# Weights in fp32 over SyncE's queue with casts on chip, in place of casting transfers from GpSimd, in a fused linear-attention and feed-forward kernel

## The chip, the cores and the metric

One Trainium2 chip, one of its cores. The metric is the device time of one execution in microseconds; a kernel's time is the median of its runs. TensorE (PE in the profile) multiplies matrices into PSUM; VectorE (DVE), ScalarE (ACT) and GpSimd (POOL) work on tiles of 128 partitions; SyncE (SP) computes nothing and issues transfers. Each of these engines takes its instructions strictly in the order in which they stand in the program: one that waits holds up all behind it. SyncE's transfers run over the queue that the page calls q1 hardware_dynamic, GpSimd's over q0 software_dynamic; both use the same 16 DMA engines. Only the transfers from GpSimd's queue change the type of the data in this kernel.

## What is computed

Gated linear attention (called GLA here) over a sequence, and a feed-forward layer on its output:

```python
# q, k, v, alpha: (4, 8, 768, 48) fp32
for t in range(S):
    state = alpha[:, :, t, :, None] * state + einsum('bhd,bhe->bhde', k[:, :, t], v[:, :, t])
    y[:, :, t] = einsum('bhd,bhde->bhe', q[:, :, t], state)
x = y.transpose(0, 2, 1, 3).reshape(3072, 384)
h = x @ w_in                 # w_in (384, 2048) fp32
r = maximum(h, 0)
out = (r * r) @ w_out        # w_out (2048, 384) fp32; out (3072, 384) fp32
```

The products are made in bf16 with sums in fp32, so both weights have to lie in SBUF as bf16: `w_in_b` (128 x 3 x 2048) and `w_out_b` (128 x 16 x 384). In HBM each is 3.15 MB of fp32.

## The kernel before, in words

The 3,072 rows are cut into 24 chunks of 128 rows, six to a sequence. For each chunk four fp32 loads of 192 KB (alpha, q, k, v: tiles `at`, `qt`, `kt`, `vt`, function `add_load`, line L290) go over SyncE's queue; each of the four tiles has six buffers, so the load of chunk s waits until chunk s - 6 has been used.

A chunk's GLA (`add_chunk`) is a chain over four engines. ScalarE takes Ln of alpha (L312); TensorE sums it over the rows (p0, `bank<-L_s,utri_b`); ScalarE makes A, its inverse and the end-of-chunk factors (L331 to L341); VectorE multiplies q and k with them (L350, L353); TensorE transposes (L220) and VectorE copies the result out (`qkT`, L307); TensorE makes the scores (`sc`), VectorE masks them (`sm`, L391, two a chunk); TensorE adds the chunk's share to the state (`st`), VectorE decays it (L411), ScalarE copies it to bf16 (`sb`, L416); TensorE makes the output (`bank<-vb,sm` and `bank<-sb,qkT`), ScalarE copies it (`xn`, L305), TensorE transposes it, and VectorE puts it into `xT_big` (L307). GpSimd casts v (`vb`, L317).

The feed-forward layer goes over groups of chunks, of 4, 1, 1, 2, 2, ... chunks. For a group and each of the 16 slices f of the hidden dimension, TensorE makes the first product from `w_in_b` (three matmuls; `add_moe1`), ScalarE the relu `r` (L490, eight buffers), VectorE the square `gT` (L497). The second product (`add_moe2`) takes `gT` and `w_out_b`, 16 matmuls for each chunk, in four quarters of four f; ScalarE or VectorE copies the result out (L527, L525) and SyncE stores it (L532). The first group starts its first four slices with three of its four chunks and adds the fourth chunk afterwards, and takes the first three quarters of the second product for all its four chunks before any last quarter. All matmuls go through one helper, L217.

The order of the instructions on each engine is written by a planner (`Plan`) when the kernel is built: every operation has an estimated duration, dependencies and a priority, and the planner puts them in the order of their planned starts. Some operations may go to the cheapest of several engines. Transfers have a planned queue of their own, `DMA`, which is served strictly in the order of adding. Changed durations thus change the order on every engine. Ahead of the first feed-forward work, gaps in TensorE's plan are filled with dummy matmuls (`bank<-warm`).

The weights come in nine pieces, `W_CUT`: w_in in slices of 2, 2, 4, 4, 4 of the 16 f, w_out in four slices of 4. Each is a transfer from GpSimd (L254, L256) that reads fp32 and writes bf16 into its place. Two kinds of holds keep the two queues apart: `hold_w` is a one-column copy on GpSimd that waits for a chunk load (q of chunk 3, later alpha of chunk 4) and so delays the weight transfers behind it, and `hold_x` is a one-column copy on GpSimd, from the first w_out piece into the alpha tile of chunk 4 (L275), for which SyncE's load of chunk 4 has to wait. The written order of loads and pieces is

```python
DMA_ORDER = [0, 1, 2, 3, "i", "i", "i", "i", "i", "o", "o", "o", 4, "o", 5]
LOAD_ORDER = {2: [(2, "at"), (2, "qt"), (2, "kt")], 3: [(3, "at"), (3, "qt"), (3, "kt"), (2, "vt"), (3, "vt")]}
HOLD_W = {3: "qt", 4: "at"}
HOLD_X = {4: ("o", 0)}
```

Of the kernel before, what the change touches and what calls it, by code (L numbers as in the profile page):

```python
# [8 lines left out]
FP32 = mybir.dt.float32  # L9
# [130 lines left out]
def kernel(  # L140
# [10 lines left out]
    nc = tc.nc  # L151
    B, H, S, D = q.shape
    HD = H * D
    P = 128
# [3 lines left out]
    d_model, d_ff = moe_w_in.shape  # L158
    n_tok = out.shape[0]
    KT = d_model // P  # L160
# [5 lines left out]
    w_in_r = moe_w_in.rearrange("(j p) f -> p j f", p=P)  # L166
    w_out_r = moe_w_out.rearrange("(j p) n -> p j n", p=P)
    out_r = out.rearrange("(tt p) n -> tt p n", p=P)

    consts = ctx.enter_context(tc.tile_pool(name="consts", bufs=1))  # L170
    big = ctx.enter_context(tc.tile_pool(name="big", bufs=1))
    LB = 6
    loads = ctx.enter_context(tc.tile_pool(name="loads", bufs=LB))
    work = ctx.enter_context(tc.tile_pool(name="work", bufs=4))
    rpool = ctx.enter_context(tc.tile_pool(name="rpool", bufs=8))
    opool = ctx.enter_context(tc.tile_pool(name="opool", bufs=6))

    ps_sc = ctx.enter_context(tc.tile_pool(name="ps_sc", bufs=1, space=PSUM))
    ps_st = ctx.enter_context(tc.tile_pool(name="ps_st", bufs=1, space=PSUM))
# [11 lines left out]
        out=utri_f, in_=utri_f, compare_op=ALU.is_ge, fill=0.0,  # L191
# [7 lines left out]
    w_in_b = consts.tile([P, KT, d_ff], BF16)  # L199
    w_out_b = consts.tile([P, FT, d_model], BF16)  # L200
# [12 lines left out]
    def pin(ins):  # L213
        tc.keep_in_program_order(ins)
# [18 lines left out]
        return banks[i].tile(shape, dt, name=f"bank{i}")  # L233
    X_SLACK = 0.2
    LD = 0.93
    WLD = 2.05
    SQ_PRIO = 0.0

    def add(eng, dur, emit, *deps, **kw):
        return plan.add(Op(eng, dur, emit, deps, **kw))  # L240

    w_ready = {"i": [], "o": []}
    W_CUT = {"i": [0, 2, 4, 8, 12, 16], "o": [0, 4, 8, 12, 16]}
    W_ISSUE = 0.78
    hold = consts.tile([P, 1], FP32)

    def load_w(which):
        j = len(w_ready[which])
        lo, hi = W_CUT[which][j:j + 2]

        def e_issue():
            if which == "i":
                sl = slice(lo * P, hi * P)
                pin(nc.gpsimd.dma_start(out=w_in_b[:, :, sl], in_=w_in_r[:, :, sl]))  # L254
            else:
                pin(nc.gpsimd.dma_start(out=w_out_b[:, lo:hi, :], in_=w_out_r[:, lo:hi, :]))  # L256
        issue = add("POOL", W_ISSUE, e_issue, w_gate[0], prio=-3.0, lat=0.4)
        w_ready[which].append(add("DMA", WLD * (hi - lo) / 4, lambda: None, issue, lat=2.2))

    def w_dep(which, f):  # L260
        return w_ready[which][[hi > f for hi in W_CUT[which][1:]].index(True)]

    w_gate = []

    def hold_w(d, nm):
        def e_hold():
            pin(nc.gpsimd.tensor_copy(hold, d[nm][:, 0, 0:1]))
        w_gate[:] = [add("POOL", 0.3, e_hold, d["ld_" + nm], prio=-6.0)]

    def hold_x(d, which, f):  # L270
        src = w_in_b[:, 0, f * P:f * P + 1] if which == "i" else w_out_b[:, f, 0:1]

        def e_hold():
            d["at"] = loads.tile([P, H, D], FP32, name="at")
            pin(nc.gpsimd.tensor_copy(d["at"][:, 0, 0:1], src))  # L275
        d["go"] = add("POOL", 0.3, e_hold, w_dep(which, f), prio=-6.0)

    C = [dict() for _ in range(NT)]
    state = {}
# [3 lines left out]
    def add_load(s, nm):  # L283
        d = C[s]
        b, c = divmod(s, NCH)

        def ld():
            if nm not in d:
                d[nm] = loads.tile([P, H, D], FP32, name=nm)
            pin(nc.sync.dma_start(out=d[nm], in_=SRC[nm][b, c]))  # L290
        prev = C[s - LB]["use_" + nm] if s >= LB else None
        d["ld_" + nm] = add("DMA", LD, ld, prev, d.get("go") if nm == "at" else None, lat=2.0 if s < 4 else 2.4, at=0.6)

    def add_chunk(s):
        d = C[s]
# [239 lines left out]

    DMA_ORDER = [0, 1, 2, 3, "i", "i", "i", "i", "i", "o", "o", "o", 4, "o", 5]
    LOAD_ORDER = {2: [(2, "at"), (2, "qt"), (2, "kt")], 3: [(3, "at"), (3, "qt"), (3, "kt"), (2, "vt"), (3, "vt")]}
    HOLD_W = {3: "qt", 4: "at"}
    HOLD_X = {4: ("o", 0)}
    for d in DMA_ORDER + [s for s in range(NT) if s not in DMA_ORDER]:  # L540
        if d in ("i", "o"):
            load_w(d)
        else:
            if d in HOLD_X:
                hold_x(C[d], *HOLD_X[d])
            for s, nm in LOAD_ORDER.get(d, [(d, nm) for nm, _ in srcs]):
                add_load(s, nm)
            if d == 3:
                add_chunk(2)
            if d != 2:  # L550
                add_chunk(d)
            if d in HOLD_W:
                hold_w(C[d], HOLD_W[d])
    b1 = b2 = None
    SPLIT_F = 4
    FIRST_PARTS = [[0, 1, 2], [3]]
# [38 lines left out]
    for op in plan.order:  # L595
        if op.eng == "PE":
# [3 lines left out]
            if pe_end is not None and DUMMY:  # L600
                n = max(0, int((op.start - pe_end - 0.2) / 0.11))
# [34 lines left out]
```

## Time and profile before

| | |
|---|---|
| runs | 195.91, 196.31, 198.04 us; median 196.31 |
| span of the profiled execution | 195.5 us, first to last instruction; the runs lie 0.4 to 2.5 us above it |
| TensorE busy | 183.6 us, 94% |
| VectorE, ScalarE busy | 133.8 us, 68%; 131.2 us, 67% |
| GpSimd busy | 24.9 us, 13% |
| q1 (SyncE) | 23.60 MB, its packets 55.7% of the 16 engines' span |
| q0 (GpSimd) | 3.15 MB as written (bf16), 11.5% |
| HBM read | 25.17 MB |
| DMA share by fortieths of the span | `6999999999989999989999968531101011011122`: nearly full until about 125 us, then low |

The page has no separate time for the profiled execution besides its span, so a sum is made on the span and set beside the runs. Busy time is the union of an engine's instructions; the share of the span is an average over stages that are limited by different things, so the prediction reads stretches of time as well as totals. A row of a timeline gives start, length, engine, line, operation, tiles written and read, shapes, and in brackets the idle time ahead of it with what ended it. A row of the chain gives start, length and what the time was spent on. A row of a stretch gives its bounds and length, each engine's busy time with its number of instructions (PE, PEld, DVE, ACT, POOL), the granted clock, the share of the DMA engines and the rate in GB/s.

### The profile page before, as it was taken

Reading aid. Unit: us, or ns where it says so; the run is one execution under the profiler, and the core shown is the slowest. Engines: PE = TensorE matmul, PEld = TensorE weight load, DVE = VectorE, ACT = ScalarE, POOL = GpSimd, SP = SyncE. Lnnn points to the kernel's source line nnn. Section 1 sums busy time; section 2 is a strip of 40 time slices with the busy share of each in tenths; the row PEclk is TensorE's granted clock in tenths of the full one; section 3 lists DMA queues with packets and bytes.
Section 4 is the critical chain, followed back from the end, with each engine's and each line's share of the span. In section 5 each row is a group of like instructions: output and inputs, shape, how many; then the busy total and the mean of one; then the engine's idle time right before and its main releaser. Section 6 shows DMA issues by size and latency. Waiting matters only on the chain.

```text
span 195.5 us, 5263 instructions
## 1 busy us (share of the span) xinstructions
PE 183.6 (94%) x1957; PEld 132.6 (68%) x1957; DVE 133.8 (68%) x367; ACT 131.2 (67%) x384; POOL 24.9 (13%) x49
## 2 busy tenths in 40 slices
PE   7788899999989999979999999999999999999993
PEld 3466654566776787766777777777777778767661
DVE  0687866255997899858967857668879968743300
ACT  3565679328897799666887866867787657646410
POOL 5128700201111121311111011011010000000000
PEclk9999999999999999999999999999999999999999
DMA  6999999999989999989999968531101011011122
GB/s 127 226 211 163 112 189 206 194 191 212 261 160 205 191 219 198 212 169 210 236 196 231 198 135 181 127 82 40 40 5 40 3 40 44 0 42 41 42 80 82
DMA packets 107434, 27.08 MB, mean 139 GB/s; under 512 B 100368, under 2 KB 107408, under 8 KB 107408
## 3 DMA queue, kind: packets, MB, share of 16 engines
q1 hardware_dynamic: 103296, 23.60, 55.7%
q0 software_dynamic: 4112, 3.15, 11.5%
q8 instruction: 15, 0.25, 0.5%
q14 instruction: 11, 0.09, 0.1%
HBM read 25.17 MB, written 4.72 MB: 153 GB/s over the span
## 4 chain that ended last, share of the span: by engine, by line
PE 63%; DMA 13%; DVE 7%; SPq 6%; ACT 4%; POOL 3%; issue 2%; ACTq 0%; POOLq 0%
PE bank L217 55%; DMA w_out_b<-in_moe_w_out_dram 7%; SPq L290 6%; PE bank L220 4%; DMA vt<-in_v_dram 4%; DMA at<-in_alpha_dram 3%; DVE sm L391 3%; PE sc L217 3%; DVE gT L497 2%; ACT r L490 1%; POOL w_in_b L254 1%; ACT ob L527 1%; PE st L217 1%; POOL vb L317 1%; DVE st L411 1%
## 5 line engine op out<-in xcount | busy, mean ns | idle before, releaser
L490 ACT ACTIVATE r<-bank 128x256 bf16<-128x256 f32 (+3 forms) x196 | 67.8, 383 | 24.0 <-PE bank L217 21.1
L217 PE MATMUL bank<-xT_big,w_in_b 128*128 128x256 bf16 (+3 forms) x588 | 81.1, 270 | 2.7 <-ACT r L490 2.5
L217 PE MATMUL bank<-w_out_b,gT 128*128 128x384 bf16 x384 | 74.0, 326 | 0.4 <-DMA w_out_b<-in_moe_w_out_dram 0.3
L497 DVE TENSOR_TENSOR gT<-r 128x256 bf16<-128x256 bf16 (+3 forms) x196 | 49.7, 286 | 23.4 <-ACT r L490 22.6
L217 PEld LDWEIGHTS <-w_in_b 128*128 128x128 bf16 x588 | 49.6, 97 | 16.3 <-issue 3.7
L217 PEld LDWEIGHTS <-gT 128*128 128x128 bf16 x384 | 36.4, 98 | 18.0 <-DVE gT L497 0.5
L391 DVE TENSOR_TENSOR sm<-sc,utri_b 128x512 bf16<-128x512 f32 x48 | 30.8, 684 | 3.9 <-PE sc L217 3.8
L317 POOL CAST vb<-vt 128x384 bf16<-128x384 f32 x24 | 14.5, 606 | 101.4 <-PE bank L217 50.8
L350 DVE TENSOR_TENSOR qA_s<-qt,A 128x384 bf16<-128x384 f32 x24 | 13.6, 566 | 11.7 <-ACT A L331 11.5
L307 DVE COPY qkT<-bank 128x1024 bf16<-128x1024 bf16 (+1 forms) x27 | 16.6, 618 | 5.8 <-PE bank L220 5.6
L312 ACT ACTIVATE L_s<-at 128x384 bf16<-128x384 f32 x24 | 12.6, 524 | 7.4 <-DMA at<-in_alpha_dram 7.1
L527 ACT COPY ob<-bank 128x384 f32<-128x384 f32 x21 | 10.1, 479 | 10.7 <-PE bank L217 10.5
L331 ACT ACTIVATE A<-bank 128x384 bf16<-128x384 f32 x24 | 11.8, 492 | 7.5 <-PE bank L217 7.5
L217 PEld LDWEIGHTS <-qkT 64*128 64x128 bf16 (+1 forms) x272 | 10.9, 95 | 8.7 <-DVE gT L497 3.1
L305 ACT CAST xn<-bank 128x384 bf16<-128x384 f32 x24 | 11.5, 481 | 6.7 <-PE bank L217 6.5
L353 DVE TENSOR_TENSOR kI_s<-kt,Ainv 128x384 bf16<-128x384 f32 x24 | 13.7, 572 | 0.1
L416 ACT CAST sb<-st 128x384 bf16<-128x384 f32 x20 | 9.6, 480 | 3.6 <-DVE st L411 3.1
L217 PE MATMUL bank<-warm 128*128 128x256 bf16 (+1 forms) x57 | 10.6, 316 | 1.5 <-DVE ae_s L210 1.3
L335 ACT ACTIVATE Ainv<-bank 128x384 bf16<-128x384 f32 x24 | 11.9, 496 | 0.0
L411 DVE TENSOR_TENSOR st<-st,ae_s 128x384 f32<-128x384 f32 x20 | 11.1, 556 | 0.3 <-PE st L217 0.2
L307 DVE COPY xT_big<-bank 128x384 bf16<-128x384 bf16 x23 | 8.1, 351 | 3.8 <-PE bank L220 3.7
L217 PE MATMUL bank<-vb,sm 128*128 128x48 bf16 x192 | 9.6, 184 | 1.1 <-DVE sm L391 0.9
(42 smaller groups left out, 131.8 us busy)
## 6 DMA issues: line engine op xcount, KB each, us to landing
at<-in_alpha_dram SPq DMA_DIRECT2D x24, 192.0 KB, 3.8
qt<-in_q_dram SPq DMA_DIRECT2D x24, 192.0 KB, 3.7
kt<-in_k_dram SPq DMA_DIRECT2D x24, 192.0 KB, 3.7
vt<-in_v_dram SPq DMA_DIRECT2D x24, 192.0 KB, 3.8
out_dram<-ob SPq DMA_DIRECT2D x24, 192.0 KB, 2.3
w_out_b<-in_moe_w_out_dram POOLq DMA_DIRECT2D x4, 384.0 KB, 11.0
w_in_b<-in_moe_w_in_dram POOLq DMA_DIRECT2D x3, 384.0 KB, 7.2
w_in_b<-in_moe_w_in_dram POOLq DMA_DIRECT2D x2, 192.0 KB, 4.2
```

The lines of the kernel that those rows point to most:

```text
L217: pin(nc.tensor.matmul(*a, **kw))
L307: pin(nc.vector.tensor_copy(out_t, in_t))
L312: pin(nc.scalar.activation(L[:, :, 0:D], d["at"], AF.Ln))
L317: pin(nc.gpsimd.tensor_copy(d["vb"], d["vt"]))
L335: pin(nc.scalar.activation(d["Ai"], d["pm"][:, 0:HD].rearrange("p (h d) -> p h d", h=H), AF.Exp, scale=-1.0))
L350: pin(nc.vector.tensor_mul(qA[:, :, 0:D], d["qt"], d["A"]))
L353: pin(nc.vector.tensor_mul(kI[:, :, 0:D], d["kt"], d["Ai"]))
L391: pin(nc.vector.tensor_mul(d["sm"][:, hh], d["sc"][:, hh], utri_b.to_broadcast([P, NP, P])))
L411: pin(nc.vector.tensor_mul(st4, st4, bcast(ae, D)))
L490: pin(nc.scalar.activation(box["r"][:, 0:n], box["ph"][:, 0:n], AF.Relu))
L497: pin(nc.vector.tensor_mul(gT[g][:, f, lo * P:lo * P + n], box["r"][:, 0:n], box["r"][:, 0:n]))
L527: pin(nc.scalar.copy(box["ob"], box["po"]))
```

## The change

The nine pieces become plain fp32 transfers on SyncE's queue into a pool of four staging tiles, in the written order with the chunk loads. A cast on chip, which the planner gives to GpSimd, VectorE or ScalarE by its estimate, writes the bf16 weights; what used a piece now depends on its cast. The transfer of a piece waits for the cast of the piece four before it, whose staging tile it takes. Both holds are gone. The planner's estimates for a piece and for later chunk loads change.

```diff
+    stage = ctx.enter_context(tc.tile_pool(name="stage", bufs=4))
...
-    WLD = 2.05
+    LD1 = 0.98
+    WLD = 2.1
...
+    w_cast = []
     W_CUT = {"i": [0, 2, 4, 8, 12, 16], "o": [0, 4, 8, 12, 16]}
-    W_ISSUE = 0.78
-    hold = consts.tile([P, 1], FP32)
+    SB = 4

     def load_w(which):
         j = len(w_ready[which])
         lo, hi = W_CUT[which][j:j + 2]
+        n = hi - lo
+        box = {}
+        if which == "i":
+            src, dst = w_in_r[:, :, lo * P:hi * P], w_in_b[:, :, lo * P:hi * P]
+            shape = [P, KT, n * P]
+        else:
+            src, dst = w_out_r[:, lo:hi, :], w_out_b[:, lo:hi, :]
+            shape = [P, n, d_model]

         def e_issue():
-            if which == "i":
-                sl = slice(lo * P, hi * P)
-                pin(nc.gpsimd.dma_start(out=w_in_b[:, :, sl], in_=w_in_r[:, :, sl]))
+            box["w"] = stage.tile(shape, FP32, name=f"w{which}{n}", tag="stage")
+            pin(nc.sync.dma_start(out=box["w"], in_=src))
+
+        def e_cast():
+            if op.eng == "POOL":
+                pin(nc.gpsimd.tensor_copy(dst, box["w"]))
+            elif op.eng == "DVE":
+                pin(nc.vector.tensor_copy(dst, box["w"]))
             else:
-                pin(nc.gpsimd.dma_start(out=w_out_b[:, lo:hi, :], in_=w_out_r[:, lo:hi, :]))
-        issue = add("POOL", W_ISSUE, e_issue, w_gate[0], prio=-3.0, lat=0.4)
-        w_ready[which].append(add("DMA", WLD * (hi - lo) / 4, lambda: None, issue, lat=2.2))
+                pin(nc.scalar.copy(dst, box["w"]))
+        prev = w_cast[-SB] if len(w_cast) >= SB else None
+        ld = add("DMA", WLD * n / 4, e_issue, prev, lat=2.0)
+        op = add({"POOL": 0.1 + 0.46 * n, "DVE": 0.1 + 0.2 * n, "ACT": 0.1 + 0.32 * n}, 0, e_cast, ld, prio=-3.0)
+        w_cast.append(op)
+        w_ready[which].append(op)
...
-    def hold_w(d, nm):
...
-    def hold_x(d, which, f):
...
-        d["ld_" + nm] = add("DMA", LD, ld, prev, d.get("go") if nm == "at" else None, lat=2.0 if s < 4 else 2.4, at=0.6)
+        d["ld_" + nm] = add("DMA", LD if s < 4 else LD1, ld, prev, lat=2.0 if s < 4 else 2.4, at=0.6)
...
-    HOLD_W = {3: "qt", 4: "at"}
-    HOLD_X = {4: ("o", 0)}
...
-            if d in HOLD_X:
-                hold_x(C[d], *HOLD_X[d])
...
-            if d in HOLD_W:
-                hold_w(C[d], HOLD_W[d])
```

## The prediction

> **What bounds the kernel now.** I read the busy shares first, then idle time of TensorE by stage, then the chain and the queues behind the two places where TensorE waits.
>
> ```profile
> PE 183.6 (94%) x1957; PEld 132.6 (68%) x1957; DVE 133.8 (68%) x367; ACT 131.2 (67%) x384; POOL 24.9 (13%) x49
> ...
> PEclk9999999999999999999999999999999999999999
> ```
>
> TensorE is busy 94% of 195.5 us at an undiminished clock. Its work is the same before and after (as many matmuls, dummies included), so a change can only move the moment at which feed-forward work starts, and the holes after it. By stage (length, TensorE busy, ...):
>
> ```profile
> 40.00:50.00 10.00, 9.52 (x111) 6.49 (x110) 6.15 (x14) 6.68 (x22) 0.98 (x2) 1.00 1.02 208
> 50.00:60.00 10.00, 9.36 (x149) 7.58 (x146) 9.64 (x40) 8.52 (x37) 0.56 (x2) 1.00 0.97 210
> 60.00:80.00 20.00, 19.57 (x252) 15.55 (x249) 18.61 (x47) 17.47 (x53) 4.00 (x5) 1.00 0.98 203
> 80.00:100.00 20.00, 18.12 (x209) 13.90 (x207) 15.25 (x46) 14.28 (x43) 2.70 (x5) 1.00 1.02 205
> 100.00:120.00 20.00, 19.86 (x217) 14.78 (x214) 15.65 (x43) 15.22 (x44) 1.01 (x2) 1.00 0.94 199
> ```
>
> Holes: 0.48 + 0.64 + 0.43 + 1.88 + 0.14 = 3.57 us. In 50 to 80 the vector engine (9.64 of 10, 18.61 of 20) is the tight one. In 80 to 100 it is the transfers (share 1.02 of the DMA engines): the chain shows alpha of chunk 15 issued at 82.22, landing 5.14 us later; ScalarE waits for it at the head of its queue, relus behind it, and TensorE behind the relus:
>
> ```profile
> 82.22 5.14 DMA at<-in_alpha_dram
> ...
> 87.38 0.52 ACT L312 ACTIVATE L_s<-at 128x384 bf16<-128x384 f32 x1 [1.56 <-DMA at<-in_alpha_dram]
> ...
> 88.36 0.82 PE L217 MATMUL bank<-xT_big,w_in_b 128*128 128x256 bf16 x6 [1.49 <-ACT r L490]
> ```
>
> From chunk 12 to 15 each Ln starts as its alpha lands, so the stream of chunk loads sets that stage. It resumed late: SyncE stood still from 14.30 to 31.54 for the hold, and the third w_out piece landed at 35.16:
>
> ```profile
> 22.34 12.82 DMA w_out_b<-in_moe_w_out_dram
> ...
> 31.54 0.37 SPq L290 DMA_DIRECT2D at<-in_alpha_dram  x1
> ...
> 35.20 2.11 PE L217 MATMUL bank<-w_out_b,gT 128*128 128x384 bf16 x12 [0.29 <-DMA w_out_b<-in_moe_w_out_dram]
> ```
>
> **Part 1: the transfers.** Nine issues leave GpSimd (0.75 to 0.87 us each, 7 us) and three small holds; GpSimd keeps only its 24 vb casts. That was on the chain between chunk 2's v and w_out (17.38 to 22.34). Nine SyncE issues come in, 0.7 us each by the chunk rows. SyncE's sixteen loads are issued by 14.30 in either kernel. Alpha of chunk 3, issued at 9.66, landed 4.0 later, at 13.7; four more follow at 0.87 us each (the step of the landings before it), so the last v lands near 17.1, against 18.0 where the other queue's first pieces ran beside it.
>
> How long is an fp32 piece of 768 KB on this queue? No row shows it. Lower bound: on the old queue the first w_out piece ended GpSimd's wait at 31.25 and the third landed at 35.16, so 1.95 us each. Upper bound: chunk loads, 192 KB per 0.87 us, give 3.5 us; these are 192-byte packets, the pieces rows of 1 to 2 KB. The last five pieces took (35.16 - 24.52) / 5 = 2.13 (24.52: issue at 17.83 plus 6.7). I take 2.1, the same source rows. The Trainium skill, "DMA: Bandwidth & Descriptors", Specifications, gives about 358 GB/s of HBM to one core, which would be 2.2 us a piece by estimate and move chunk 4 later by 0.7; the 1.95 us measured is 403 GB/s, so the trace speaks against that limit.
>
> Landings then: the two half pieces at 18.2 and 19.2, the rest of w_in at 21.3, 23.4, 25.5, w_out at 27.6, 29.7, 31.8; chunk 4 from 32.7 to 35.3 (35.9 to 38.8 before), the last w_out at 37.4 (43.4), chunk 5's v at 40.9 (45.5), chunk 6's alpha at 41.8 (46.1). The stream is 3 to 4 us ahead. Piece n + 4 waits on SyncE for the cast of piece n, and the chunk loads queue behind it; by the cast times below each cast ends before its successor's turn, so the queue does not run dry.
>
> **Part 2: the casts.** In the built order two (768 elements) stand on ScalarE behind chunk 2's state copy, seven (1,536 elements) on VectorE: one ahead of chunk 3's xT copy, five among the sixteen squares of the first group, one in chunk 4. ScalarE: Ln of 384 elements takes 0.52, relu grows by (597 - 281) / 384 = 0.82 ns an element, so 0.85 each. VectorE has no such copy. Its copies:
>
> ```profile
> L307 DVE COPY qkT<-bank 128x1024 bf16<-128x1024 bf16 x20 | 13.7, 687 | 4.5 <-PE bank L220 4.5
> ...
> L307 DVE COPY qkT<-bank 128x512 bf16<-128x512 bf16 x7 | 2.9, 421 | 1.3 <-PE bank L220 1.2
> L525 DVE COPY ob<-bank 128x384 f32<-128x384 f32 x3 | 1.7, 554 | 0.0
> ```
>
> The bf16 copies grow by 0.52 ns an element: 0.687 + 512 x 0.52 = 0.95 us. The fp32 copy out of PSUM is 554 where bf16 of that length is 351, so 1.05 ns an element: 0.554 + 1,152 x 1.05 = 1.76 us. I take 0.95, the row of the same output type and nearest length, and keep 1.76 as the upper end. "VectorE: DVE Perf Modes", the perf-mode tier table, gives an fp32 copy with both ends in SBUF twice the rate of one that touches PSUM. By it the ob row would not apply (estimate 0.8 us of streaming) and the forecast stands; by the row alone the kernel would be slower; no run here shows which.
>
> **Part 3: along the path, at 0.95.** GpSimd's issues beside VectorE go away: kI_s at 18.90 took 0.85 instead of 0.55, qA_s 0.69. Chunk 2's last product stands ahead of chunk 3's transposes in the new order and starts near 18.5 instead of 19.44, when the mask multiply (17.08 + 1.29) is done. ScalarE's two casts then run from 20.2 to 21.9, and the first feed-forward matmul starts near 21.1 (21.55 before). The gain is taken back: three relus stand ahead of chunk 3's xn (24.0), and the third cast ahead of its xT copy: 23.5 to 24.45, copy to 24.75, feed-forward of that chunk from 24.85 (24.76 before).
>
> From there VectorE runs without pause: two squares of 384 (0.6), one of 128 (0.2), cast to 26.55, three squares (0.45), one of 512 (0.42), cast to 28.35, three squares, cast to 30.55, four squares, cast to 33.2, three squares, cast to 35.4. In the first group the second product reaches its third quarter at 34.7 and needs that last cast (f 8 to 11): it goes on at 35.45, where before it went on at 35.20. So +0.25. The state multiply of chunk 4 waits for the ninth cast; 8 matmuls (1.3 us) of the second product stand ahead of its next product, which hides that at 0.95 us and exposes up to 0.5 at 1.76.
>
> After that: no cast is left beyond chunk 4. With alpha of chunk 15 landing 3 to 4 us earlier the 1.56 us wait on ScalarE ends before it begins, so I give back the hole of 80 to 100, 1.88 us. What is late next there is VectorE, 15.25 of 20 busy, no bound. The other 1.69 us lie mostly where VectorE is full; an earlier stream does not fill those, and I keep them. Sum: +0.25 - 1.88 = -1.6 us; span 195.5 to 193.9. The page's execution lies 0.4 below the lowest run (195.91) and 0.8 below the median, and I count from the median: 196.31 - 1.6 = **194.7 us**.
>
> **Rivals.**
> - **A rate of one element (slower).** Casts at 1.76 us. Chunk 3's xT ends at 25.55 (+0.8), five casts add 4.0 to VectorE's run, and the third w_out piece is cast at 40.2 instead of 35.4: +5.0 against before at the first group's second product; with 1.88 given back 196.3 + 3.1 = 199.4. VectorE has slack of only 0.22 us a square there (idle ahead of each 512-wide square), so each tenth on a cast costs TensorE about 0.6; it decides from about 1.2 us a cast. For it: ob's 554. Against: PSUM is not in the cast.
> - **All holes close.** GLA of chunks 4 to 6 stands earlier in the new TensorE order, and takes vector work into 40 to 50, where VectorE was 6.15 of 10 busy. Then 3.57 - 0.25 = 3.3: 193.0.
> - **Nothing comes of the lead.** SyncE also waits for buffers (gT rows: 5.4 us in 80 to 90); chunk s needs chunk s - 6 consumed, and VectorE sets that pace, or the rewritten order opens holes as large as those closed. 196.5.
> - **Slow pieces.** 3.5 us each: w_out's third piece lands 10 us later, at 41.7; +7 less what the cover of chunk 4 gives: 202 or more.
> That the change doesn't do what it says has no chance: in the built program GpSimd has no transfer left and SyncE holds the nine pieces in the written order.
>
> **How the numbers follow.** Forecast 0.40 (194.0 to 195.6), all holes 0.20, nothing 0.20, slow casts 0.15, slow pieces 0.05. One per cent (2 us, about what the measurement can tell from no change: runs span 195.9 to 198.0) puts the borders at 194.35 and 198.27. Faster: 0.20 and 0.40 of the forecast, 0.36. Slower: 0.15 + 0.05, and 0.02 of bad order, 0.22. Within: 0.42. The range takes in 193.0 and 199.4 and leaves the slow pieces out.
>
> **What would show it.** VectorE rows named for the staging tiles at 0.9 to 1.0 us (right) or 1.7 (rival); SyncE's alpha of chunk 4 landing near 32.7; the first wait of the second product ending near 35.4; no 1.5 us hole near 85; holes of 40 to 120 near 1.7. Wrong if VectorE's squares or chunk 3's xT queue behind a cast that waits for its landing, or if SyncE's issues wait for casts so long that the DMA share falls in 20 to 35.

## The result

The changed kernel takes 204.21 us (median of 4 runs, 203.17 to 204.85) where the kernel before takes 196.11 in the runs beside it: 1.040 times as long, 95% interval 1.0345 to 1.0448. That is about 8 us slower, where 1.6 us faster was forecast, and outside the range given. The profiled execution has a span of 203.1 us; it is the slowest of the four runs (204.85).

### The profile after

The page's busy line and clock line, and the row of SyncE's queue (packets, MB, share of 16 engines' span):

```profile
PE 187.3 (92%) x1956; PEld 134.6 (66%) x1957; DVE 141.0 (69%) x375; ACT 132.3 (65%) x385; POOL 16.5 (8%) x37
...
PEclk9999999999998599999999999999999999999999
...
q1 hardware_dynamic: 107408, 29.89, 72.0%
```

VectorE gained 7.2 us (141.0 against 133.8); its seven casts take 9.0. TensorE gained 3.7 us with the same matmuls, and the clock line says why for most of it: one stretch of 6.8 us, from about 60 us on, at half the clock, worth about 3.4 us (an estimate, half of its length). The stretches of time (bounds, length, then PE, PEld, DVE, ACT, POOL busy, granted clock, DMA share, GB/s):

```profile
40.00:50.00 10.00, 10.00 (x96) 6.39 (x95) 5.50 (x10) 4.66 (x14) 1.01 (x2) 1.00 1.22 219
50.00:60.00 10.00, 9.01 (x150) 7.49 (x149) 9.12 (x30) 8.48 (x34) 1.26 (x2) 1.00 1.02 234
60.00:80.00 20.00, 17.25 (x202) 13.54 (x200) 14.67 (x48) 12.88 (x44) 2.03 (x4) 0.83 1.09 183
80.00:100.00 20.00, 19.98 (x226) 15.13 (x224) 17.23 (x50) 15.95 (x49) 3.59 (x5) 1.00 1.11 190
100.00:120.00 20.00, 19.99 (x219) 15.01 (x217) 16.32 (x46) 15.13 (x46) 1.20 (x3) 1.00 1.16 205
```

The hole of 80 to 100 is gone (19.98 busy, 18.12 before), as forecast. In its place 60 to 80 lost 2.75 us to holes, at a mean clock of 0.83. Ahead of that the start is late at three places that the prediction had named. Timeline of TensorE (start, length; in brackets the idle time ahead and what ended it): the first feed-forward matmuls, those of chunk 3, and the third quarter of the second product:

```profile
23.58 1.15 PE L218 MATMUL bank<-xT_big,w_in_b 128*128 128x384 bf16 x6 [1.34 <-ACT w_in_b L271]
...
28.14 1.02 PE L218 MATMUL bank<-xT_big,w_in_b 128*128 128x128 bf16 x12 [0.79 <-DVE xT_big L310]
...
39.12 1.14 PE L218 MATMUL bank<-w_out_b,gT 128*128 128x384 bf16 x6 [0.88 <-DVE w_out_b L269]
```

Before they stood at 21.55, 24.76 and 35.20: 2.0, 3.4 and 3.9 us earlier. Groups of the rows that write the two weights (min/median/max ns, first and last start, shapes):

```profile
L269 DVE CAST w_in_b<-wi x3: 1745/1745/1747, 26.1 to 31.4; 128x1536 bf16<-128x1536 f32 x3
L271 ACT CAST w_in_b<-wi x2: 831/832/832, 22.7 to 23.8; 128x768 bf16<-128x768 f32 x2
...
L269 DVE CAST w_out_b<-wo x4: 951/953/954, 34.0 to 43.9; 128x1536 bf16<-128x1536 f32 x4
```

The w_out casts take the forecast's 0.95 us, those of w_in nearly twice that, at the same count of elements and the same types. And the hole near 63 us, in the timeline:

```profile
61.34 0.45 ACT L493 ACTIVATE r<-bank 128x128 bf16<-128x128 f32 x2 [0.19 <-DVE gT L500]
...
62.03 0.30 ACT L493 ACTIVATE r<-bank 128x128 bf16<-128x128 f32 x1
...
62.20 0.56 DVE L353 TENSOR_TENSOR qA_s<-qt,A 128x384 bf16<-128x384 f32 x1 [0.68 <-ACT A L334]
...
62.67 1.28 DVE L394 TENSOR_TENSOR sm<-sc,utri_b 128x512 bf16<-128x512 f32 x2
...
63.87 0.55 DVE L356 TENSOR_TENSOR kI_s<-kt,Ainv 128x384 bf16<-128x384 f32 x1
...
64.33 1.03 DVE L500 TENSOR_TENSOR gT<-r 128x128 bf16<-128x128 bf16 x7
64.67 0.61 ACT L493 ACTIVATE r<-bank 128x128 bf16<-128x128 f32 x3 [1.95 <-DVE gT L500]
65.00 0.48 PE L218 MATMUL bank<-xT_big,w_in_b 128*128 128x128 bf16 x3 [2.27 <-ACT r L493]
...
67.33 1.45 PE L218 MATMUL bank<-w_out_b,gT 128*128 128x384 bf16 x4
```

VectorE does four chunk operations (qA_s, two sm, kI_s) ahead of seven squares. All eight relu tiles hold results that wait for those squares, ScalarE waits 1.95 us for a free tile, and TensorE 2.27 us for a relu, from 62.7 to 65.0. Within that hole the clock is halved, from 64.2 to 71.0: four matmuls of the second product take 1.45 us there, 0.81 elsewhere. The mean granted clock is 0.983 in this execution and 0.992 in the other three, which would be about 3.2 us at half speed (an estimate, 0.008 x 202 / 0.5).

Three more facts come from the trace's single transfers and the built programs. The chunk loads land every 1.05 us from the second on (3.71, 5.11, 6.14, 7.19, ...), about every 0.90 before; their 192-byte packets take 18.5 ns on average, 15.5 before. The `hold` column that was removed occupied 32 bytes of every partition: all tiles behind it moved by 32, so that the load tiles start at 32 more than a multiple of 64, and no longer at a multiple of 64. And the queue ran out of work behind the weights: SyncE's issue of chunk 4's k load lasted until 37.20, just ahead of the landing of the third w_out piece at 37.40, and for a microsecond the DMA engines were almost idle (the row of the issue, then the stretch from 37 to 38):

```profile
33.88 3.31 SPq L293 DMA_DIRECT2D kt<-in_k_dram  x1
...
37.00:38.00 1.00, 1.00 (x8) 0.61 (x7) 1.00 (x4) 0.57 (x1) 0.00 (x0) 1.00 0.16 33
```

### The profile page after: what moved, and what is told of

The parts are those of the page before. It is cut to its first block, busy times and chain, and to the rows that moved or that the text cites. A ratio compares the mean times of both kernels' runs of the same rounds, so it can differ in the third digit from the quotient of the medians.

```text
span 203.1 us, 5248 instructions
## 1 busy us (share of the span) xinstructions
PE 187.3 (92%) x1956; PEld 134.6 (66%) x1957; DVE 141.0 (69%) x375; ACT 132.3 (65%) x385; POOL 16.5 (8%) x37
## 4 chain that ended last, share of the span: by engine, by line
PE 72%; DVE 11%; SPq 8%; DMA 3%; ACT 3%; issue 1%; ACTq 0%; DVEq 0%
PE bank L218 62%; SPq L293 8%; PE bank L221 6%; DVE gT L500 3%; DMA wi<-in_moe_w_in_dram 3%; PE sc L218 3%; DVE w_in_b L269 2%; DVE sm L394 2%; DVE w_out_b L269 1%; PE st L218 1%; ACT ob L530 1%; ACT r L493 1%; DVE qkT L310 1%; DVE kI_s L356 0%; ACT A L334 0%
## 5 line engine op out<-in xcount | busy, mean ns | idle before, releaser
L493 ACT ACTIVATE r<-bank 128x256 bf16<-128x256 f32 (+3 forms) x196 | 68.8, 385 | 28.7 <-PE bank L218 23.0
L218 PE MATMUL bank<-w_out_b,gT 128*128 128x384 bf16 x384 | 75.1, 330 | 1.1 <-DVE w_out_b L269 0.9
L320 POOL CAST vb<-vt 128x384 bf16<-128x384 f32 x24 | 13.8, 574 | 132.5 <-DMA vt<-in_v_dram 70.8
L530 ACT COPY ob<-bank 128x384 f32<-128x384 f32 x20 | 9.6, 479 | 11.9 <-PE bank L218 11.9
L218 PE MATMUL bank<-warm 128*128 128x256 bf16 (+1 forms) x57 | 11.2, 333 | 1.4 <-DVE ae_s L211 1.2
L221 PE MATMUL bank<-ident_bf,kI_s 128*128 128x128 bf16 x96 | 9.5, 223 | 0.9 <-DVE qkT L310 0.5
```

The costliest lines, as they stand in the source:

```text
L218: pin(nc.tensor.matmul(*a, **kw))
L221: pin(nc.tensor.transpose(*a))
L320: pin(nc.gpsimd.tensor_copy(d["vb"], d["vt"]))
L493: pin(nc.scalar.activation(box["r"][:, 0:n], box["ph"][:, 0:n], AF.Relu))
```

## The experiments

Each kernel was compared with runs of the kernel before on the same chip: the first four kernels shared 7 runs (median 195.85), the next four 31 (196.61), the last two 19 on a slower chip (198.36). Across these groups only the ratios compare, and such a comparison takes it that a chip slows both kernels alike. Code is shown against the changed kernel unless it says otherwise. "Third quarter" is that of the second product in the first group. The "0.87 us" of the expectations is the prediction's step between landings.

### The 32 bytes: three kernels

The changed kernel with the column put back, unused; line added:

```diff
     w_out_b = consts.tile([P, FT, d_model], BF16)
+    pad = consts.tile([P, 1], FP32)
```

> The changed kernel with one unused 4-byte column put back where the hold's column stood, so that every tile behind it, the load tiles among them, moves up by 32 bytes and starts on a multiple of 64 again, as in the kernel before. Instructions and their order are untouched. Theory A (address): the chunk loads are slow because their tiles start at 32 modulo 64. Then landings step by 0.87 us again instead of 1.05, the 192-byte packets take 15 ns nearly all, chunk 2's v lands near 17.3 instead of 19.3, the first feed-forward matmul starts near 21.8 instead of 23.6, and the kernel takes 198.5 to 201 us. Theory B (the fp32 pieces or the placement in HBM slow the loads): no change, 203 to 205 us.

Measured 202.10 us (200.93 to 202.80), ratio 1.032 (1.025 to 1.039). Packets of 192 bytes take 15.7 ns again, and the queue's row falls from 72.0%:

```profile
q1 hardware_dynamic: 107408, 29.89, 64.7%
```

The first feed-forward matmul starts at 20.83 without a wait and the third quarter at 36.33, yet the hole near 60 us stayed:

```profile
62.50 0.48 PE L219 MATMUL bank<-xT_big,w_in_b 128*128 128x128 bf16 x3 [2.47 <-ACT r L494]
```

The kernel is 2.1 us faster by the medians and 1.5 by the ratios, whose intervals overlap.

The same line added to the kernel before, where `hold` still stands, moves its tiles the other way:

> The kernel before with one more unused 4-byte column beside the hold's, so that all tiles behind it start 32 bytes further, at 32 modulo 64. Nothing else differs: the weights still come from GpSimd. Theory A (address): landings step by 1.05 us, a quarter to a third of the 192-byte packets take more than 15 ns, the stream of chunk loads reaches chunk 15 five to eight us later, and the kernel takes 198 to 202 us. Theory B (fp32 pieces or HBM): 196 us, no change.

Measured 201.19 us (200.31 to 201.59), ratio 1.027 (1.021 to 1.034). In the kernel before, 32 bytes of address alone cost 5.3 us. The packets took 18.4 ns, and alpha of chunk 15 landed at 91.3 in place of 87.4. The profiled run (201.59) has a half clock for 3.4 us, but the other three, at 0.997 or more, still took 200.31 to 201.27. A row of the page:

```profile
q1 hardware_dynamic: 103296, 23.60, 64.1%
```

(55.7% for the same packets before.) The third shifts only the tiles allocated behind the load tiles, in the kernel before:

```diff
+    pad = work.tile([P, 1], FP32, name="pad", bufs=1)
     ps_sc = ctx.enter_context(tc.tile_pool(name="ps_sc", bufs=1, space=PSUM))
```

> The kernel before with the unused column placed behind the pool of load tiles, so that the load tiles keep their addresses and only the tiles that the engines write (A, vb, sm, xn, r, ob) start 32 bytes further. If the start of the load tiles is what counts: 196 us, steps of 0.87 us, packets of 15 ns. If the engines' own tiles were what slowed the shifted kernel: 200 us or more.

Measured 196.75 us, ratio 0.999 (0.994 to 1.004): no difference. It is where the load tiles start that counts, not the addresses of the tiles that the engines compute on.

### The slow w_in casts: two kernels

In the changed kernel a w_in piece goes into three runs of 512 elements with gaps, because `w_in_b` is laid out by the three k blocks. Here `w_in_b` lies piece by piece, and a cast writes one run:

```diff
-    w_in_b = consts.tile([P, KT, d_ff], BF16)
+    w_in_b = consts.tile([P, KT * d_ff], BF16)
...
-            src, dst = w_in_r[:, :, lo * P:hi * P], w_in_b[:, :, lo * P:hi * P]
+            src, dst = w_in_r[:, :, lo * P:hi * P], w_in_b[:, KT * lo * P:KT * hi * P].rearrange("p (j f) -> p j f", j=KT)
...
-                mm(prog_t[:, 0:n], lhsT=w_in_b[:, j, f * P:(f + 1) * P], rhs=xT_big[:, j, t0:t0 + n],
+                mm(prog_t[:, 0:n], lhsT=w_in_slice(j, f), rhs=xT_big[:, j, t0:t0 + n],
```

> The changed kernel with w_in laid out piece by piece in SBUF, so that each cast of w_in writes one contiguous run of 1,536 elements instead of three runs of 512 with gaps. Order of instructions unchanged, addresses of all other tiles unchanged. Theory C (the three w_in casts run at half rate because of the gaps in what they write): they take 0.95 us like the w_out casts instead of 1.75; chunk 3's xT copy and all that follows comes 0.8 us earlier, the third quarter of the second product 0.8 to 1.2 earlier (the landing of the third w_out piece at 37.4 then holds it), and the kernel takes 202.5 to 203.5 us. Rival (w_in comes out slower for its source or destination tile as such): casts stay at 1.75 us and the time at 204.

Measured 203.60 us (201.51 to 204.24), ratio 1.038 (1.028 to 1.047). The casts are as fast as those of w_out:

```profile
L269 DVE CAST w_in_b<-wi x3: 954/959/961, 25.2 to 30.1; 128x1536 bf16<-128x1536 f32 x3
```

So the 1,745 ns come from the shape of what is written. The Trainium skill, "VectorE: DVE Perf Modes", section "What auto-detection actually checks", says that a one-source operation in SBUF gets the double rate when the outermost dimensions above 1 of source and destination are both even, or equal. In the built program the source is one run of 1,536 and the destination 3 x 512: 3 is odd and not 1,536. The two durations agree with that rule; whether the gaps alone, with an even number of runs, would cost anything was not tried. In time the difference to the changed kernel is 0.6 us by the medians, with overlapping intervals; with the pad as well:

> The changed kernel with both: the column put back and w_in contiguous. If A and C are all that is wrong with the prediction: casts 0.95 us, loads in steps of 0.87, third quarter of the second product at about 35.5, and 194 to 196.5 us. If the rewritten order itself costs time (the hole of 2.3 us at 62.7 and the half clock behind it): 198 us or more with both repaired.

Measured 201.54 us (199.66 to 202.42), ratio 1.029 (1.021 to 1.036), 0.6 below the kernel with the pad alone on the same chip, with overlapping intervals: unclear, 1 us at most. The address is again worth 2.1 us by the medians (203.60 to 201.54), again with overlapping intervals. The third w_out piece lands at 36.27, the third quarter starts at 37.30, and a hole of 2.35 us, from 62.0 on, stays.

### The relu tiles: two kernels

The last kernel with twelve relu tiles in place of eight:

```diff
-    rpool = ctx.enter_context(tc.tile_pool(name="rpool", bufs=8))
+    rpool = ctx.enter_context(tc.tile_pool(name="rpool", bufs=12))
```

> The changed kernel with the column put back, w_in contiguous, and twelve buffers for the relu tile instead of eight; the order of instructions stays. Theory D (the hole of 2.35 us at 62 stands because ScalarE has filled all eight relu tiles while VectorE, in its new order, does a whole chunk's qA, both masks and kI ahead of seven squares): the hole shrinks to under 0.8 us, TensorE no longer idles over 1.5 us in one piece there, the half clock after it is rarer, and the kernel takes 198 to 199.5 us against 201.5. Rival (VectorE is simply full there, and TensorE must wait for it wherever the buffers stand): the hole moves or splits, 201 to 202 us.

Measured 198.81 us (198.37 to 199.30), ratio 1.010 (1.007 to 1.014), against 1.029: 3.5 us by the ratios, and the intervals lie apart. In the timeline of TensorE the hole has shrunk to

```profile
58.74 0.33 PE L219 MATMUL bank<-xT_big,w_in_b 128*128 128x128 bf16 x3 [0.45 <-ACT r L500]
...
62.67 0.81 PE L219 MATMUL bank<-w_out_b,gT 128*128 128x384 bf16 x4 [0.64 <-ACT r L500]
```

and the granted clock of all ten runs is 0.996 or more (0.983 to 0.992 in the four of the changed kernel). Twelve relu tiles in the kernel before:

> The kernel before with twelve relu buffers. Theory D says that only the new order runs out of relu tiles: 195.5 to 196.3 us, no difference. If relu tiles were short in the old order too, it is up to 1 us faster.

Measured 196.47 us, ratio 1.002 (0.997 to 1.007). The old order never ran out of relu tiles; it is the rewritten order that needs more.

### The last per cent: three kernels

These start from the kernel with pad, contiguous w_in and twelve relu tiles. In it the planner still reckons with pieces that land earlier than they do. First its latency of a piece is doubled, which changes the order only:

```diff
-        ld = add("DMA", WLD * n / 4, e_issue, prev, lat=2.0)
+        ld = add("DMA", WLD * n / 4, e_issue, prev, lat=4.0)
```

> As the one with twelve relu buffers, but the planner is told that a piece lands 2 us later (latency 4.0 instead of 2.0), so that it places casts and what depends on them nearer to where the pieces land on the chip (the third w_out piece lands at 36.3, the plan had it at 32.2). Theory E (an order made for landings 4 us too early costs time, as casts and first-group squares block VectorE and ScalarE): 1 us or more faster than with twelve buffers alone. Rival (the pieces themselves are late, the order matters little): within 0.7 us of it.

Measured 198.83 us, ratio 1.009 (1.005 to 1.014): the same. Next comes the third w_in cast, which stands ahead of chunk 3's `xT_big` copy on VectorE and so causes a TensorE gap of 0.90 us in the kernel with twelve relu tiles:

```profile
25.77 0.44 PE L219 MATMUL bank<-xT_big,w_in_b 128*128 128x128 bf16 x5 [0.90 <-DVE xT_big L317]
```

It is made to follow that copy:

```diff
-        op = add({"POOL": 0.1 + 0.46 * n, "DVE": 0.1 + 0.2 * n, "ACT": 0.1 + 0.32 * n}, 0, e_cast, ld, prio=-3.0)
+        op = add({"POOL": 0.1 + 0.46 * n, "DVE": 0.1 + 0.2 * n, "ACT": 0.1 + 0.32 * n}, 0, e_cast, ld, C[3]["x"] if which == "i" and j == 2 else None, prio=-3.0)
```

> The kernel of e5_r12, with the third w_in cast made to stand behind chunk 3's xT copy in VectorE's order, so that the copy no longer waits for that cast. Theory V (casts on VectorE ahead of chunk 3 cost the time): the TensorE gap of 0.90 us at 24.9 us closes and the kernel is 0.6 to 0.9 us faster than e5_r12: 197.9 to 198.2. Theory L (the landing of the w_out pieces sets the first group's end): the gap closes, but the second product still reaches its third quarter near 36.1 and waits there longer; time 198.5 to 199.1, as e5_r12 (198.81).

Measured 199.48 us where the kernel before takes 198.36: ratio 1.005 (1.001 to 1.010). By the ratios that is 1.0 us better, near the 0.6 to 0.9 of theory V, but the intervals overlap. The gap closed, and no wait took its place. Timeline of TensorE:

```profile
25.75 1.02 PE L219 MATMUL bank<-xT_big,w_in_b 128*128 128x128 bf16 x12
26.61 0.38 PE L219 MATMUL bank<-warm 128*128 128x256 bf16 x2
27.05 7.93 PE L219 MATMUL bank<-xT_big,w_in_b 128*128 128x512 bf16 x36
34.82 2.97 PE L219 MATMUL bank<-w_out_b,gT 128*128 128x384 bf16 x16
```

The wait at the third quarter that theory L expected is absent: sixteen matmuls of the second product follow each other.

Last, the w_out pieces are made half as large, from the kernel with twelve relu tiles. Each half is cast twice, so that the casts stay about as long in all (eight of 0.55 us in place of four of 0.95). This kernel leaves out half of w_out:

```diff
-            src, dst = w_out_r[:, lo:hi, :], w_out_b[:, lo:hi, :]
-            shape = [P, n, d_model]
+            src, dst = w_out_r[:, lo:lo + 2, :], w_out_b[:, lo:hi, :]
+            shape = [P, 2, d_model]
...
-                pin(nc.vector.tensor_copy(dst, box["w"]))
+                for d in ([dst] if which == "i" else [dst[:, 0:2, :], dst[:, 2:4, :]]):
+                    pin(nc.vector.tensor_copy(d, box["w"]))
```

> The kernel of e5_r12, with each w_out piece loading only two of its four row blocks (384 KB instead of 768 KB); the two blocks are cast twice, so that the casts keep their total length. It leaves out half of the content of w_out. Theory L (landings of w_out): the third w_out piece lands near 31 to 32 instead of 35.1, the third quarter of the second product starts near 35.2 (0.9 us earlier), chunk 4 and later load 3 to 4 us earlier, time 197.4 to 198.2. Theory V (casts and order on VectorE): the pieces land earlier, the third quarter moves by 0.3 us at most, time 198.5 to 199.1, as e5_r12 (198.81).

Measured 197.96 us (197.41 to 198.68) beside 198.36, ratio 0.999 (0.996 to 1.002): level with the kernel before, 2.3 us better by the ratios than with whole pieces. The third w_out piece landed at 32.45 (with whole pieces 35.11), chunk 4's alpha at 33.2 (35.7), chunk 5's at 38.5 (42.3). Yet neither theory has it right: the third quarter did not come earlier (no wait, but its ninth matmul starts near 36.3, an estimate from the row of sixteen; 36.15 with whole pieces). TensorE's busy time says where its profile gained, in 40 to 60 (with whole pieces, then with half pieces):

```profile
40.00:60.00 20.00, 18.17 (x250) 13.43 (x247) 15.29 (x42) 13.91 (x51) 2.00 (x3) 1.00 0.94 203
```

```profile
40.00:60.00 20.00, 18.63 (x261) 14.03 (x259) 16.73 (x44) 14.11 (x54) 2.23 (x4) 1.00 0.87 186
```

This points to the chunk loads behind w_out, those of chunks 4 to 6, rather than to the second product. It is read from one profile of each, on two chips; the spans differ by 0.7 us and the ratios by 2.3, so it is not settled which part of the 2.3 us this is. The kernel with the cast behind the copy, on the same chip and with whole pieces, lies between the two:

```profile
40.00:60.00 20.00, 18.38 (x256) 13.74 (x253) 16.47 (x43) 13.91 (x51) 1.73 (x3) 1.00 0.97 212
```

No kernel here beats the kernel before; the best of those that compute everything is at 1.005 of it.

## Why the prediction was wrong

The loss of about 8 us, by the steps between the ratios: the 32 bytes 1.5 us (2.1 by the medians, twice; the intervals overlap), the half-rate casts about 0.6 (unclear), the relu tiles with the halved clock 3.5 (clear), and 2 us that remain at a ratio of 1.010 and whose cause is open.

- **"Four more follow at 0.87 us each"** failed. The step of the loads was carried over from the kernel before as if the removed hold cost nothing but its time. It was also 32 bytes ahead of the load tiles, and without them a load takes 1.05 us: the v of chunk 3 was due at 17.1 and landed at 19.92. No rival had it. Alone, in the kernel before, it costs 5.3 us; here 1.5 to 2.1, presumably since other waits cover a part. With the pad the last v still landed at 17.6 to 18.3, because a gap stands between q and k of chunk 3. The prediction put that lateness down to GpSimd's pieces ("ran beside it"), but the gap is there with and without them: 14.54 to 16.77 in the kernel before, 14.41 to 16.81 with pad, one-run casts and twelve relu tiles.
- **Pieces of 2.1 us** held: 2.03 us each for w_in's last two in the changed kernel, 2.13 each over the last five up to the third w_out piece in the kernel with twelve relu tiles (24.47 to 35.11). "Slow pieces" is out.
- **"The queue does not run dry"** failed, at both ends of the weights. At the head, in the kernel with twelve relu tiles, w_in's first three pieces landed at 19.19, 21.28 and 24.47, where 18.2, 19.2 and 21.3 were reckoned: 3.2 us lost, 1.0 of them already in the last chunk load, and the third w_out piece at 35.1 instead of 31.8. SyncE's issue of the first piece took 2.29 us there (at 14.23); in the changed kernel it is a v load that took 1.86, with 0.99 and 1.00 for the two loads ahead of it. Transfers of 16 KB on the instruction queue lie beside both (at 14.1), but whether they cause it was not tried. At the tail, the issue of chunk 4's k ended within 0.3 us of the third w_out piece's landing in every kernel here, the kernel before among them; it took 3.3 us behind whole pieces in the changed order, 1.8 behind half pieces. The loads behind it were then not yet queued, and the DMA share fell to 0.16 for a microsecond in the changed kernel (0.70 at that place in the kernel before). So the promised lead of 3 to 4 us was never there: chunk 4's alpha landed at 35.0 with the pad, 36.8 with pad and one-run casts, and 35.7 with twelve relu tiles as well, against 35.9 before.
- **Casts at 0.95 us** held for w_out (0.953) and on ScalarE (0.832, forecast 0.85). For w_in the upper end of 1.76 was the right one (1.745), for a reason outside the argument: not the type and not PSUM, but the shape of the destination. The rival put 3.1 us on all casts at that rate; with six of the nine at the forecast's rate or better, it was about 0.6 (unclear).
- **The path**: 21.1, 24.85 and 35.45 were forecast; with the pad, 20.83 for the first matmul, and 36.33 for the third quarter. The order of the steps was right, the last 0.9 late; in the changed kernel itself they stand at 23.58, 28.14 and 39.12. The cast ahead of chunk 3's copy was named and held to be harmless (24.85 against 24.76); in the kernel with pad, one-run casts and twelve relu tiles the piece landed so late that TensorE waited 0.90 us there.
- **"No cast is left beyond chunk 4 ... no bound"** is the step that cost most. The stretch after 50 us was priced by the engines' busy shares alone; the rewritten order was not followed there. Its VectorE takes four chunk operations ahead of seven squares, eight relu tiles do not cover that, and the hole brings a halved clock. Twelve tiles in place of eight took 3.5 us back. The prediction had "the rewritten order opens holes" as half a sentence in a rival whose price was next to nothing, and gave "bad order" 0.02 on the slow side.
- **The hole of 80 to 100** did close, as forecast, but its 1.88 us were not to be had in full. In all later runs of the kernel before, the time is the span plus 2.0 us, so the profiled execution of span 195.5 took about 197.5, more than the median of 196.31. The kernel with the pad behind the load tiles, which takes the same time as the kernel before, was profiled in its fastest run (194.89 us, span 192.8), and there the stretch is full:

```profile
80.00:100.00 20.00, 19.95 (x226) 15.54 (x224) 16.83 (x48) 16.30 (x49) 2.51 (x5) 1.00 0.99 197
```

  The kernel before with twelve relu tiles, as fast as the kernel before, was profiled at a span of 195.0 us (197.09, above its median), and there 1.25 us are missing:

```profile
80.00:100.00 20.00, 18.75 (x214) 14.33 (x212) 15.91 (x48) 14.73 (x44) 2.52 (x5) 1.00 1.01 202
```

  The hole belonged in its full size to a slower execution; taking all of it off the median was wrong. Even with all faults mended and half of w_out not loaded, the kernel is level: "nothing comes of the lead" (196.5) was the rival nearest to the mended kernel.

## What to carry to other kernels

Removing or adding even a 4-byte tile moves every tile allocated behind it: compare the start addresses of the load destinations and the mean time of their packets before reading anything else in the trace. Where a planner rewrites the order, follow the new order through the stages far from the edit, and set the number of buffers of each hand-over against the longest run of other work ahead of its consumer. And before giving a hole back, find out from the runs' spans whether the profiled execution is a typical one.

## What the runs showed of the hardware

- Loads of 192-byte rows into tiles that start at 32 more than a multiple of 64: 18.1 to 18.5 ns a packet, 1.05 us for 192 KB in the first ten loads; at a multiple of 64, 15.5 to 15.7 ns and 0.89 to 0.93 us (0.99 in the two profiles on the slower chip). Of the packets 29 to 33% take over 15 ns in the one case, 1 to 4% in the other. Why was not tested.
- In a TensorE hole of 2.27 us the clock fell to half, 1.4 us after the hole's start, and stayed there for 6.8 us; with the pad alone, and with one-run casts alone, for 3.4 us. The Trainium skill, "TensorE: Matmul & The Clock Gate", section "HAM oscillation — how this bites in real kernels", warns of gaps of more than about 3.4 us; here a shorter one was enough, though not in every run: of the four runs of the kernel with pad and one-run casts, whose profile has a hole of 2.35 us, two have a granted clock of 0.999 or 1.0 and took 199.66 and 201.39 us, the other two 0.99 and took 201.68 and 202.42.
- A cast of 1,536 fp32 elements between SBUF tiles on VectorE: 0.95 us into one run, 1.745 us into three runs of 512. On ScalarE 768 elements take 0.83 us into one run and into three runs of 256.
- The time exceeds the span by 2.0 to 2.1 us for the kernels with transfers from GpSimd and by 1.7 to 1.8 us for those without: 0.3 us in favour of the change that no profile shows.
